# Linear attention and a gated channel mix: the branch to the general path in front of the last two downs, one store per tile, and the first cast of v on other engines

## The chip, the cores and the metric

The kernel runs on one core of a Trainium2 chip. The metric is device time in microseconds (us) of one execution. A core has TensorE (PE, with its weight loads as PEld), VectorE (DVE), ScalarE (ACT), GpSimd (POOL) and SyncE (SP), each with a sequencer of its own that works through its instructions in order, and 16 DMA engines behind queues. In this kernel the big transfers are issued by SP.

## The reference

```python
# q, k, v: (8, 8, 576, 64) float32
q_s = softmax of q over the last axis          # exp(q - max) / sum
k_s = softmax of k over axis 2 (the sequence)
kv  = einsum('bhsd,bhse->bhde', k_s, v)
att = einsum('bhsd,bhde->bhse', q_s, kv)
x   = att.transpose(0, 2, 1, 3).reshape(8, 576, 512)
x_prev = x shifted by one position, zeros first
xk = mu_k * x + (1 - mu_k) * x_prev
xr = mu_r * x + (1 - mu_r) * x_prev
k  = maximum(xk @ w_k, 0)                      # (512, 1024)
v  = k * k @ w_v                               # (1024, 512)
r  = 1 / (1 + exp(-(xr @ w_r)))                # (512, 512)
out = r * v                                    # (8, 576, 512) float32
```

## The kernel before

There are 8 batches. Each batch goes through attention in two units of four heads: `load` of q, k and v (SP), `exp` of q and k (ACT), a cast of v to bf16 (`cast_v`), `sum_q` and `scale_q` (DVE), a transpose of q (by TensorE in the first two batches, by DMA later), `kv` and `x` (TensorE). For the first two batches the mixing weights are folded into the small kv matrix (`weigh_kv`, `x_mixed`, `evict_mixed`); for the others ACT and DVE do the shift and the mix (`shift_x`, `mix_x`). Then follow eight `up` steps per batch (128 features each, 8 matmuls), `relu` on ACT and `square` on ACT or DVE.

The output is made in pairs of batches, 4 pairs of 9 tiles (i, m), 128 rows by 512 columns each: `gate` (4 matmuls) with `tanh` on ACT, `down` (8 matmuls of 512 columns), `finish` on DVE, which multiplies the two into an output buffer `ot` (four of these), and `store` to HBM. Tile m = 4 of each pair holds the last 64 rows of one batch and the first 64 of the next. The last tile, (3, 8), is made in two halves of 256 columns. Accumulators of gates and downs share two buffers of PSUM (`one`).

The kernel skips subtracting the maximum before the exponentials. To be safe, it keeps the reciprocals of all sums in `inv`; `watch` counts on DVE those that lie between 1e-6 and 1e6, `gather` adds the counts by one small matmul, `judge` writes a flag, and `read_flag` loads it into a register of every engine. If a sum was out of range, all engines run `general()`, which does the whole computation again with the maxima subtracted; otherwise all engines jump over it. With the given inputs they jump. The jump is a compare-and-branch on each of the five sequencers; a prefetch hint for it is given at the program's start to the engines named in `mark_branch_hint_location`. Behind a branch an engine that jumped raises the semaphores that its part of the general path would have raised, so that later waits hold on both paths: each engine its own, and SP also those of the eight lanes over which the DMAs' semaphores go round.

The order of the work is written by a planner. The class `Plan` holds steps with an engine (or a choice of engines), a cost and a due time; it plays them through once and calls the steps' functions in the order of their planned starts. A table `SHIFTS` moves every step's due time, and `FIXED` pins some steps to an engine. Idle stretches of TensorE ahead of the first up are filled with `warm` matmuls. In the kernel before, the plan holds all downs and finishes. The last three tiles, called `LATER`, are stored behind the branch, and the branch stands behind everything else:

```python
    with tc.manual_schedule():
        pl.emit(("PE", 0.3, warm, ev["mup"], ev["up", 0, 0]))
        kept, slot = {("ot", *t): slot[("ot", *t)] for t in LATER}, Turns()
        slot.update(kept)
        with tc.If(st["bad"] != 0, preferred_fallthrough_block=True, label="general"):
            general()
        for t in LATER[:-1]:
            store(*t)
        for a in range(2):
            store(*LAST, (nc.sync, nc.scalar)[a], a)
```

Each `store` issues two DMAs of 64 rows. In the program's view of the changed kernel, the lines of the kernel are ten later at the front and up to 25 later at the end.

Of the kernel before, what the change touches and what calls it, by code (L numbers as in the profile page):

```python
# [10 lines left out]
ACT = mybir.ActivationFunctionType  # L11
# [11 lines left out]
-371 1633 2839 -359 6 -1821 -1 -304 3 72 -1538 -534 1385 822 386 1069 -2408 351 589 -649 -354  # L23
-2035 -676 -1613 84 2123 10 -534 -412 -25 -715 1916 -1725 -252 -583 -1817 -117 -752 329 -1136
992 961 677 -574 918 969 976 964 799 489 1060 918 899 960 1082 774 1283 758 736 1180 1358 1293
1147 1581 1449 458 1496 286 1228 1220 169 640 -286 -1128 -413 488 -1330 2596 -2246 -36 -1916
-587 -1383 -627 -498 539 859 1579 -494 1647 1856 345 957 2374 2099 -212 -469 -542 -1593 -544
-554 -64 -295 1476 -1579 -769 -366 -57 119 2187 -967 -615 -1616 395 -602 -3116 894 1329 906 176
1387 -4293 -42 -1020 1086 -2414 311 41 -306 1796 -2617 -3490 -377 -1313 -483 304 -157 -580 -251
-1948 -1869 -2051 -642 149 -1242 -447 112 -849 -2 -546 1212 -853 2304 -589 -455 -286 1353 -1236  # L30
126 -562 -1050 1419 -1647 275 -2047 -660 -2500 -1185 577 -845 -1119 665 541 518 -756 -278 -1809
747 -877 -2031 -467 1876 271 253 -608 -548 -1112 464 -568 -2071 -169 -1882 706 2652 320 -1180 50
-763 -1899 -847 -829 -547 335 -849 -1767 -1763 -1098 -424 -649 -201 459 -745 -1690 -320 -820
-1995 -2164 -141 779 -1519 996 796 263 961 -59 1472 749 1415 -1972 -2090 -987 -620 -143 837 1067
-67 813 516 183 1210 2280 -70 331 -995 1225 195 894 -1462 -25 1058 937 1209 384 -49 1172 1035
1165 967 1477 1807 981 -920 626 -422 2118 -1017 386 -684 1275 736 75 273 -221 -481 86 1590 1303
-768 1234 1613 2230 -1042 681 1411 -307 -389 886 -849 -427 1883 1145 -1070 278 -1072 895 -1821
-1804 1691 586 -600 -1426 -198 454 -1280 -299 1282 1334 -313 707 -1680 -335 -292 -474 796 1620
-263 23 1272 -357 1598 1064 -2901 -390 -2837 1326 -552 -1417 -200 -419 -226 1844 -3 -102 1195
628 354 543 -339 -913 1764 -1857 334 -3424 1373 1829 541 1472 653 901 441 1138 1771 -699 -694  # L40
-560 -1258 -707 1375 602 679 361 1851 612 -1386 -856 -529 294 1595 1043 -473 93 178 -592 135
-1788 99 -4132 955 953 517 1107 -1189 -1541 -3341 284 309 981 980 813 -584 -979 329 -416 -2743
-2298 -1498 -1654 -358 -1383 -1214 -4023 -572 -785 1013 -1457 1502 275 -1354 497 -2225 -388 -830
-401 -573 -172 -1671 -199 -924 -1162 -439 -2067 -806 -292 745 -1209 754 923 -667 349 622 -831
2024 266 -1483 -875 172 818 -838 -727 340 2219 1365 1198 1033 1354 -1181 2156 -519 1317 -774 615
-987 1621 84 1079 830 -945 1156 2076 254 -1771 919 -426 955 1153 -2552 721 -1882 678 855 -1245
-2372 -3135 -3280 1036 1245 388 382 775 986 -1530 -1449 1294 -186 674 -1282 437 -1007 56 -1372
671 569 -3033 1345 -1017 -1146 810 -3295 -213 -2650 1308 -450 -1041 340 1045 -415 -3330 640 -280
-1558 -1620 -1082 1329 -273 1404 1142 -331 -57 -789 -782 2497 -445 -258 276 264 -941 -1029 -903
389 1131 455 378 324 1297 1045 1425 88 -373 1103 131 396 273 29 601 1511 -359 1645 -212 376 1318  # L50
-1239 289 39 1764 1345 -998 2961 -1552 -1875 -618 -1758 1360 1000 -546 182 1835 1436 916 -448
-1361 1710 850 1177 -509 -394 -1154 596 1040 -147 752 584 461 448 179 2019 848 772 2104 434 1490
-577 500 -380 721 1242 -644 -203 -840 -1264 790 1323 800 1249 -1395 -3082 -102 1148 907 303 911
819 1034 230 1083 859 -1270 1178 857 1389 -1029 -3290 871 -1391 658 -2200 -1108 -1167 -1593 674
-151 -2322 1468 -666 788 1148 -2079 -964 583 -1436 -1585 712 -2742 -3491 -3982 708 -4466 -3011
-129 1128 -218 -717 -866 -600 530 -2508 -2780 -447 -1911 346 791 -1290 -435 -1268 -229 355 -3522
-4279 75 -737 -3082 1775 -897 -3480 -1190 1067 666 -937 475 21 -740 -16 -506 315 464 -193 -2109
-809 1236 843 -723 -1841 1711 670 1539 -9997977 -9998081 -9998655
"""
FIXED = {s: e for e, steps in {  # L60
    "DVE": (31, 142, 153, 168, 180, 199, 206, 208, 420, 423, 426, 429, 435, 441, 444, 453,
        456, 465, 468, 474, 480, 486, 501, 504, 507,),
    "ACT": (151, 156, 162, 166, 172, 181, 185, 191, 204, 438, 447, 471, 492, 495, 498,),
    "POOL": (33, 34, 138, 157, 175, 194,),
# [3 lines left out]
class Plan:  # L68
# [12 lines left out]
    def step(self, eng, cost, due, fn=None, after=(), uses=(), lat=0.12):  # L81
        s = {"eng": eng if isinstance(eng, dict) else {eng: cost}, "due": due, "fn": fn,
             "n": len(self.steps), "lat": lat, "uses": [], "left": 0, "next": [], "fix": None}
        self.steps.append(s)
        self.link(s, after, uses)
        return s
# [78 lines left out]
    def emit(self, fill=None):  # L165
        order = self.run()
        if fill:
            eng, gap, fn, first, last = fill
            t, more = first["start"] + first["cost"] + 1.0, []
            for s in [s for s in order if s["on"] == eng]:  # L170
                while first["start"] < s["start"] <= last["start"] and t + gap < s["start"]:
                    more.append({"start": t, "fn": fn, "eng": {eng: gap}, "on": eng})
                    t += gap
                t = max(t, s["start"] + s["cost"])
            order = list(heapq.merge(order, more, key=lambda s: s["start"]))
        for s in order:
            if s["fn"]:
                s["fn"](s["on"]) if len(s["eng"]) > 1 else s["fn"]()
# [3 lines left out]
def kernel(  # L182
# [335 lines left out]
    LATER = [(B // 2 - 1, m) for m in (J - 3, J - 2, J - 1)]  # L518
# [14 lines left out]
    def store(i, m, eng=None, a=None):  # L533
        c0, c1 = (0, C) if a is None else (a * C // 2, (a + 1) * C // 2)
        for h in range(2):
            blk = 2 * m + h
            b, jj = 2 * i + blk // J, blk % J
            (eng or nc.sync).dma_start(
                out=bass.AP(tensor=out.tensor, offset=out.offset + (b * S + jj) * C + c0,
                            ap=[[J * C, 64], [1, c1 - c0]]),  # L540
                in_=at("ot", i, m)[64 * h:64 * h + 64, c0:c1])
# [17 lines left out]

    def read_flag():  # L560
# [3 lines left out]
            "general", "LikelyTaken", engines=[mybir.EngineType.SP, mybir.EngineType.Activation])  # L564
# [99 lines left out]
    for n in range(B):  # L664
        for u in range(2):
# [7 lines left out]
            if n < NM:  # L673
                vc = [pl.step({"ACT": 0.6, "POOL": 0.68, "DVE": 0.65}, 0, LATE,
# [57 lines left out]
    for b in range(B):  # L732
        mixed = [ev["mix", b, u, 0, c] for u in range(2) for c in range(2)]
        relus = []
        for f in range(FT):
# [5 lines left out]
            if f % 2:  # L741
# [3 lines left out]
                relus = []  # L745
    for i in range(B // 2):
        for m in range(J):
# [9 lines left out]
            for a in ((None,) if (i, m) != LAST else (0, 1)):  # L757
                s, z = sl("one", "vp", i, m, a), 1.0 if a is None else 0.5
                p = pl.step("PE", z * T_DOWN, d, lambda i=i, m=m, a=a: down(i, m, a),
                            after=[*ev["wv"], *squares], uses=[sl("k2", i), s], lat=0.2)  # L760
                ev["fin", i, m, a] = p = pl.step(
                    "DVE", 0.6 * z, d + 1.7 * z, lambda i=i, m=m, a=a: finish(i, m, a),
                    after=[p, t], uses=[s, th, ot])
                d += 0.9
            if (i, m) not in LATER:
                pl.step("DMA", 1.0, d + 1.5, lambda i=i, m=m: store(i, m), after=[p], uses=[ot],
                        lat=2.0)

    d = due["down", B // 2 - 1, J - 3]
    a = pl.step("DVE", 1.2, d - 6.0, watch, after=[ev["mix", B - 1, u, 0, h]  # L770
                                                   for u in range(2) for h in range(2)])
    a = pl.step("PE", 0.2, d - 4.0, gather, after=[a], uses=[sl("two", "flag")], lat=0.2)
    a = pl.step("DVE", 0.2, d - 3.0, judge, after=[a], uses=[sl("two", "flag")])
    a = pl.step("PE", 0.1, d, read_flag, after=[a])
    for t in LATER:
        pl.step("DMA", 0.0, LATE, after=[a, *(s for k, s in ev.items()
                                              if k[0] == "fin" and k[1:3] in LATER)],
                uses=[sl("ot", *t)])
# [34 lines left out]
    def general():  # L813
        for i in range(B // 2):
# [26 lines left out]
            for m in range(J):  # L841
                gate(i, m)
                tanh(i, m)
                down(i, m)
                finish(i, m)
                if (i, m) not in LATER:
                    store(i, m)

    with tc.manual_schedule():
        pl.emit(("PE", 0.3, warm, ev["mup"], ev["up", 0, 0]))  # L850
        kept, slot = {("ot", *t): slot[("ot", *t)] for t in LATER}, Turns()
        slot.update(kept)
        with tc.If(st["bad"] != 0, preferred_fallthrough_block=True, label="general"):
            general()
        for t in LATER[:-1]:
            store(*t)
        for a in range(2):
            store(*LAST, (nc.sync, nc.scalar)[a], a)
# [30 lines left out]
```

## Time and profile before

| what | before |
|---|---|
| times of 3 runs | 208.03, 208.97, 210.22 us; median 208.97 |
| the profiled execution: its own time | 207.88 us |
| the profiled execution: span of the page | 206.0 us |
| TensorE busy | 186.6 us, 91% |
| ACT / DVE / POOL busy | 145.1 / 140.5 / 32.4 us |
| first `up` matmul starts | 20.43 us |
| last matmul ends | 196.15 us |
| DMA of the program | 46.41 MB on SP's queue, 0.14 MB on ACT's |

The page and the answers of the trace are of one execution. Times in them count from the start of the span. An engine's name with a q behind it (SPq, ACTq, DVEq, PEldq) is that engine's sequencer: rows of waits, branches, semaphores and issued DMAs, during which the engine itself may be at work. In a row of waits, "X <- Y: a, n, b" says that X waited for Y for a us in all, n times, the longest b us. In a row of the timeline the first two numbers are the start and the duration in us, and the brackets name the idle time before and what ended it.

### The profile page before, as it was taken

To read this page: it belongs to the slowest core of one execution; us is meant where nothing else is said; L and a number is where in the kernel's file an instruction comes from. 1 tells how busy PE (TensorE), PEld (TensorE's weight loads), DVE (VectorE), ACT (ScalarE), POOL (GpSimd) and SP (SyncE) were. 2 spreads that over 40 slices of the span, in tenths; PEclk is the share of its full clock that TensorE was granted. 3 is DMA by queue.
4 is the path that set the end of the run, shared out by engine and by line. 5 is a ranking of instruction groups with operands and counts; after the bars stand their busy time and mean duration, and the time that the engine had idled before them with its cause. 6 is when DMAs were issued, how large, how long until landed. Compare 5 with 4: busy or idle time off the path is not lost.

```text
span 206.0 us, 4670 instructions
## 1 busy us (share of the span) xinstructions
PE 186.6 (91%) x1883; PEld 109.6 (53%) x1883; DVE 140.5 (68%) x214; ACT 145.1 (70%) x210; POOL 32.4 (16%) x43
## 2 busy tenths in 40 slices
PE   0779998999999899999999999999999999999900
PEld 0355775664545466665556656555646567555500
DVE  2985399887979478998689989696935282443210
ACT  3745798898894889798968999969629996330100
POOL 2067425550200400220210060000000000000000
PEclk9999999999999999999999999999999999999985
DMA  5999999989989999999999999507143222243315
GB/s 207 342 400 387 392 389 389 389 258 341 265 226 306 296 362 395 335 290 286 304 354 344 244 331 155 102 11 162 40 98 75 51 51 54 51 102 75 84 34 128
DMA packets 35883, 46.90 MB, mean 228 GB/s; under 512 B 16264, under 2 KB 16528, under 8 KB 35856
## 3 DMA queue, kind: packets, MB, share of 16 engines
q1 hardware_dynamic: 35680, 46.41, 75.0%
q8 instruction: 16, 0.26, 0.6%
q10 hardware_dynamic: 176, 0.14, 0.3%
q14 instruction: 11, 0.09, 0.2%
HBM read 33.56 MB, written 9.44 MB: 209 GB/s over the span
## 4 chain that ended last, share of the span: by engine, by line
PE 74%; DMA 10%; ACT 5%; issue 2%; SPq 2%; POOL 1%; DVE 1%; ACTq 0%
PE two L490 27%; PE one L523 25%; PE one L509 14%; DMA ldv<-in_v_dram 4%; DMA ldq<-in_q_dram 4%; PE two L415 3%; DMA ldk<-in_k_dram 3%; PE two L468 2%; PE two L446 2%; SPq L365 2%; ACT rel L495 1%; POOL vb L277 1%; ACT eq L370 1%; ACT ek L370 1%; PE two L398 1%
## 5 line engine op out<-in xcount | busy, mean ns | idle before, releaser
L490 PE MATMUL two<-xk,wk_bf 128*128 128x288 bf16 x512 | 69.0, 286 | 1.0 <-ACT rel L495 1.0
L523 PE MATMUL one<-wv_bf,k 128*128 128x512 bf16 (+1 forms) x296 | 66.7, 374 | 0.0
L490 PEld LDWEIGHTS <-wk_bf 128*128 128x128 bf16 x512 | 49.6, 98 | 19.8 <-issue 1.4
L495 ACT ACTIVATE rel<-two 128x576 bf16<-128x576 f32 x64 | 41.0, 651 | 14.9 <-PE two L490 12.5
L523 PEld LDWEIGHTS <-k 128*128 128x128 bf16 x296 | 28.1, 98 | 29.8
L529 DVE SCALAR_TENSOR_TENSOR ot<-th,one 128x512 f32<-128x512 f32 (+1 forms) x37 | 24.6, 665 | 22.3 <-PE one L523 19.4
L509 PE MATMUL one<-wr_bf,xr 128*128 128x512 bf16 x144 | 36.3, 380 | 0.1
L277 POOL CAST vb<-ldv 128x1152 bf16<-128x1152 f32 (+1 forms) x19 | 21.5, 1149 | 84.4 <-DMA ldv<-in_v_dram 82.8
L476 ACT ACTIVATE aw<-two,om 128x575 bf16<-128x575 f32 x48 | 32.6, 747 | 0.2 <-PE two L468 0.2
L514 ACT ACTIVATE th<-one 128x512 f32<-128x512 f32 x36 | 21.3, 598 | 16.1 <-PE one L509 15.0
L505 DVE TENSOR_TENSOR k<-rel 128x1152 bf16<-128x1152 bf16 x22 | 17.0, 771 | 14.7 <-ACT rel L495 14.7
L380 DVE TENSOR_REDUCE rs<-eq 128x18 f32<-128x1152 bf16 x16 | 21.6, 1348 | 2.3 <-ACT eq L370 2.1
L385 DVE TENSOR_TENSOR qs<-eq,inv 128x1152 bf16<-128x1152 bf16 x16 | 22.8, 1433 | 0.1
L481 DVE SCALAR_TENSOR_TENSOR xr<-two,mu,aw 128x576 bf16<-128x576 f32 x24 | 19.3, 807 | 3.0 <-ACT aw L476 2.9
L370 ACT ACTIVATE ek<-ldk 128x1152 bf16<-128x1152 f32 x16 | 18.6, 1163 | 3.8 <-DMA ldk<-in_k_dram 3.8
L370 ACT ACTIVATE eq<-ldq 128x1152 bf16<-128x1152 f32 x16 | 18.6, 1165 | 3.7 <-DMA ldq<-in_q_dram 3.7
L481 DVE SCALAR_TENSOR_TENSOR xk<-two,mu,aw 128x576 bf16<-128x576 f32 x24 | 19.0, 806 | 3.0 <-ACT aw L476 3.0
L509 PEld LDWEIGHTS <-xr 128*128 128x128 bf16 x144 | 13.2, 98 | 12.1 <-issue 0.3
L503 ACT ACTIVATE k<-rel 128x1152 bf16<-128x1152 bf16 x10 | 11.7, 1168 | 0.3
L415 PEld LDWEIGHTS <-ek 64*64 64x64 bf16 x576 | 6.4, 113 | 5.7 <-issue 3.2
L415 PE MATMUL two<-vb,ek 64*64 64x65 bf16 x576 | 8.2, 200 | 1.0 <-POOL vb L277 1.0
L446 PE MATMUL two<-qT,kvm 64*64 64x256 bf16 (+2 forms) x160 | 6.8, 295 | 1.1 <-ACT qT L276 0.6
(52 smaller groups left out, 77.5 us busy)
## 6 DMA issues: line engine op xcount, KB each, us to landing
ldq<-in_q_dram SPq DMA_DIRECT2D x16, 576.0 KB, 7.4
ldk<-in_k_dram SPq DMA_DIRECT2D x16, 576.0 KB, 6.9
out_dram<-ot SPq DMA_DIRECT2D x70, 128.0 KB, 3.2
ldv<-in_v_dram SPq DMA_DIRECT2D x15, 576.0 KB, 6.1
k<-in_moe_w_k_dram SPq DMA_DIRECT2D x2, 1024.0 KB, 11.4
k<-in_moe_w_v_dram SPq DMA_DIRECT2D x2, 1024.0 KB, 14.4
xr<-in_moe_w_r_dram SPq DMA_DIRECT2D x1, 1024.0 KB, 15.9
ldv<-in_v_dram SPq DMA_DIRECT2D x2, 288.0 KB, 9.1
```

What stands on the lines that cost most here:

```text
L277: return {"DVE": nc.vector, "POOL": nc.gpsimd}[eng].tensor_copy(out=out, in_=in_)
L370: nc.scalar.activation(out=at("e" + n, b, u)[:].rearrange("p j (h d) -> p h j d", h=2), in_=at("ld" + n, b, u)[:].rearrange("p h (j d) -> ...
L380: nc.vector.reduce_sum(out=rs[:], in_=at("eq", b, u)[:].rearrange("p j (h d) -> p (j h) d", h=2), axis=AX.X)
L385: nc.vector.tensor_tensor(out=at("qs", b, u)[:].rearrange("p j (h d) -> p (j h) d", h=2), in0=at("eq", b, u)[:].rearrange("p j (h d) -> p ...
L476: nc.scalar.activation(out=at("aw", b, u, h, w)[:, 1:S], in_=x_of(b, u, h)[:, 1:S], func=ACT.Copy, scale=om[:, c:c + 1])
L481: nc.vector.scalar_tensor_tensor(out=blend(b, w)[:, 2 * u + h, :], in0=x_of(b, u, h)[:, 64:64 + S], scalar=mu[:, c:c + 1], in1=at("aw", b, ...
L490: nc.tensor.matmul(ps[:, a, 0:HS], lhsT=wk_bf[:, ct, 128 * f:128 * f + 128], rhs=xk[:, ct, HS * a:HS * a + HS], start=(ct == 0), stop=(ct ...
L495: nc.scalar.activation(out=at("rel", b, f // 2)[:, f % 2, :].rearrange("p (a c) -> p a c", a=2), in_=at("two", "up", b, f)[:, :, 0:HS], fu ...
L509: nc.tensor.matmul(at("one", "rp", i, m)[:], lhsT=at("xr", i)[:, ct, 128 * m:128 * m + 128], rhs=wr_bf[:, ct, :], start=(ct == 0), stop=(c ...
L514: nc.scalar.activation(out=at("th", i, m)[:], in_=at("one", "rp", i, m)[:], func=ACT.Tanh, scale=0.5)
L523: nc.tensor.matmul(at("one", "vp", i, m, a)[:, cols], lhsT=at("k2", i)[:, f, 128 * m:128 * m + 128], rhs=wv_bf[:, f, cols], start=(f == 0) ...
L529: nc.vector.scalar_tensor_tensor(out=at("ot", i, m)[:, cols], in0=at("th", i, m)[:, cols], scalar=1.0, in1=at("one", "vp", i, m, a)[:, col ...
```

## The change

Three edits, and a new order of nearly all steps, since `SHIFTS` and `FIXED` are replaced as a whole.

- The branch becomes a step of the plan. It stands behind the down of tile (3, 6) and all finishes of earlier tiles; the downs of (3, 7) and (3, 8) and the finishes and stores of all three tiles are emitted behind it. The last three tiles' tanh comes ahead of it. The general path does the last pair's first down of these tiles itself, and leaves the other two to the common end. The flag's steps get earlier due times. The hint is given to four engines.
- `store` issues one DMA per tile, where the tile lies in one batch.
- For the first unit's two half casts of v the planner's cost on GpSimd is 1.2 instead of 0.68.

```diff
 FIXED = {s: e for e, steps in {
-    "DVE": (31, 142, 153, 168, 180, 199, 206, 208, 420, 423, 426, 429, 435, 441, 444, 453,
-        456, 465, 468, 474, 480, 486, 501, 504, 507,),
...
+    "DVE": (142, 161, 172, 180, 191, 199, 210, 420, 423, 426, 432, 444, 447, 450, 456,
+        471, 474, 486, 495, 504,),
...
+        done = set()
+        for k, s in enumerate(order):
+            if s["fn"] and k not in done:
+                if s["tail"] == "first":
+                    for n in range(k + 1, len(order)):
+                        if not order[n]["tail"]:
+                            done.add(n)
+                            self.call(order[n])
+                self.call(s)
...
     def store(i, m, eng=None, a=None):
         c0, c1 = (0, C) if a is None else (a * C // 2, (a + 1) * C // 2)
-        for h in range(2):
-            blk = 2 * m + h
-            b, jj = 2 * i + blk // J, blk % J
+        runs = [(h, 1) for h in range(2)] if 2 * m + 1 == J else [(0, 2)]
+        for h, n in runs:
+            b, jj = 2 * i + (2 * m + h) // J, (2 * m + h) % J
             (eng or nc.sync).dma_start(
                 out=bass.AP(tensor=out.tensor, offset=out.offset + (b * S + jj) * C + c0,
-                            ap=[[J * C, 64], [1, c1 - c0]]),
-                in_=at("ot", i, m)[64 * h:64 * h + 64, c0:c1])
+                            ap=[[C, n], [J * C, 64], [1, c1 - c0]]),
+                in_=at("ot", i, m)[64 * h:64 * (h + n), c0:c1])
...
+    HINTED = [getattr(mybir.EngineType, e) for e in ("PE", "DVE", "Activation", "SP")]
...
         tc.mark_branch_hint_location(
-            "general", "LikelyTaken", engines=[mybir.EngineType.SP, mybir.EngineType.Activation])
+            "general", "LikelyTaken", engines=HINTED)
...
-                vc = [pl.step({"ACT": 0.6, "POOL": 0.68, "DVE": 0.65}, 0, LATE,
+                vc = [pl.step({"ACT": 0.6, "POOL": 0.68 if n + u else 1.2, "DVE": 0.65}, 0, LATE,
...
+    branch = pl.step("PE", 0.3, LATE, lambda: part())
+    branch["tail"] = "first"
...
+                late = [branch] if (i, m) in TAIL else []
+                ev["down", i, m, a] = p = pl.step(
+                    "PE", z * T_DOWN, d, lambda i=i, m=m, a=a: down(i, m, a),
+                    after=[*ev["wv"], *squares, *(late if (i, m) != TAIL[0] else [])],
+                    uses=[sl("k2", i), s], lat=0.2)
+                ev["fin", i, m, a] = f = pl.step(
                     "DVE", 0.6 * z, d + 1.7 * z, lambda i=i, m=m, a=a: finish(i, m, a),
-                    after=[p, t], uses=[s, th, ot])
+                    after=[p, t, *late], uses=[s, th, ot])
+                o = pl.step("DMA", 0.8, d + 2.5 * z,
+                            lambda i=i, m=m, a=a: store(i, m, nc.sync if a is None else nc.scalar, a),
+                            after=[f], uses=[ot], lat=2.0)
...
+    def part():
+        nonlocal slot
+        planned, slot = slot, Turns()
+        for key in (("k2", B // 2 - 1), *(("th", *t) for t in TAIL),
+                    ("one", "vp", *TAIL[0], None)):
+            slot[key] = planned[key]
+        with tc.If(st["bad"] != 0, preferred_fallthrough_block=True, label="general"):
+            general()
+        slot = planned
...
     with tc.manual_schedule():
         pl.emit(("PE", 0.3, warm, ev["mup"], ev["up", 0, 0]))
-        kept, slot = {("ot", *t): slot[("ot", *t)] for t in LATER}, Turns()
-        slot.update(kept)
-        with tc.If(st["bad"] != 0, preferred_fallthrough_block=True, label="general"):
-            general()
-        for t in LATER[:-1]:
-            store(*t)
-        for a in range(2):
-            store(*LAST, (nc.sync, nc.scalar)[a], a)
```

In the built program the last instructions of TensorE are then: gate, down (3, 6), branch, first half of down (3, 8), down (3, 7), second half of down (3, 8). In front of all, POOL casts one half of the first unit's v and ACT the other; before, POOL cast both.

## The prediction

> **What bounds the kernel now.** I read the page first, then the waits of TensorE, then the chain of waits from its end backwards, and last the sequencers' rows of the branch. The page says that TensorE is the bound:
>
> ```profile
> span 206.0 us, 4670 instructions
> PE 186.6 (91%) x1883; PEld 109.6 (53%) x1883; DVE 140.5 (68%) x214; ACT 145.1 (70%) x210; POOL 32.4 (16%) x43
> ```
>
> The 19.4 us in which it is idle lie at two places. The waits of TensorE give the inner ones, largest first:
>
> ```profile
> PE two L308 <- DVE th L302: 5.5, 1, 5.5
> PE two L490 <- ACT rel L495: 1.0, 1, 1.0
> PE two L415 <- POOL vb L277: 1.0, 1, 1.0
> PE two L398 <- DVE qs L385: 0.8, 1, 0.8
> PE two L446 <- ACT qT L276: 0.6, 1, 0.6
> ```
>
> These are the start (5.5, then 0.8 and 1.0) and two short stalls, 0.6 near 34 us and 1.0 near 66 us. From 67 us on the chain of waits is TensorE alone, one line after the other, until its last matmul ends at 196.15 us. What is left up to 206.02, 9.87 us, is idle TensorE. That end is what the change rebuilds; here is the branch at its head, for every engine (columns: count, duration in ns, first and last start in us):
>
> ```profile
> L853 SPq EVENT_SEMAPHORE  x8: 17/17/17, 193.2 to 193.7; - x8
> ...
> L853 ACTq COMPARE_BRANCH  x1: 73/73/73, 192.5 to 192.5; - x1
> ...
> L853 SPq COMPARE_BRANCH  x1: 78/78/78, 192.7 to 192.7; - x1
> L853 ACTq EVENT_SEMAPHORE  x1: 17/17/17, 193.0 to 193.0; - x1
> L853 PEldq COMPARE_BRANCH  x1: 3312/3312/3312, 194.9 to 194.9; - x1
> L853 DVEq COMPARE_BRANCH  x1: 72/72/72, 196.2 to 196.2; - x1
> L853 PEldq EVENT_SEMAPHORE  x1: 51/51/51, 198.3 to 198.3; - x1
> L853 DVEq EVENT_SEMAPHORE  x1: 21/21/21, 199.1 to 199.1; - x1
> ```
>
> The hinted engines (SP, ACT) are past the branch 0.5 us after it starts; the two without a hint need 2.9 us (DVE, 196.19 to 199.05) and 3.4 us (TensorE, 194.93 to 198.30). Behind the branch each engine raises its own semaphores, and SP those of the eight DMA lanes; each of these rows first waits for the semaphore it raises. The stores wait for DVE's:
>
> ```profile
> SPq L538 <- DVEq L853: 5.3, 1, 5.3
> L538 SPq DMA_DIRECT2D out_dram<-ot x6: 482/596/1234, 199.1 to 203.1; - x6
> DMA to landing us min/median/max: 2.0/2.5/3.3
> ```
>
> So the 9.87 us are: last finish 0.45 (to 196.60), DVE's late branch 2.5 (to 199.10), SP issuing six stores one after the other 4.0 (the last starts at 203.09), its landing 2.04 (205.13), the closing barrier 0.89 (206.02).
>
> **Part 1: branch ahead of the last two downs.** I count from A, the moment when TensorE has only these left: the last gate (0.86), the down of tile (3,6) (1.73), a half down of (3,8) (0.87), the down of (3,7) (1.73), the other half (0.87); together 6.06. Before, that was 196.15 - 6.06 = 190.09, and the span ended at A + 15.93. The built program of after gives the order: gate, down (3,6), branch, half, (3,7), half. Steps:
> - The finish of the last ordinary tile, (3,4), ends at A + 0.72 (0.03 + 0.69). This tile lies in two batches, so it still has two stores on SP: 0.75, and 0.53 later. One lands 2.36 after its start (the pair at 190.60 and 191.13: median 2.3, longest 2.4): A + 3.64.
> - SP's row for the DMA lanes waits until this store has landed; its lane comes first, and the eight rows take 0.53 from first to last (193.20 to 193.73): A + 4.2. The finish of (3,6) on DVE overwrites a buffer that the general path also stores from, so it waits for four lanes, the last of the eight included. It runs from 4.2 to 4.9, not from 2.6.
> - Queued behind it: TensorE's down of (3,7), which takes the accumulator that this finish frees. TensorE could start it at 3.9 (gate and down 2.59; the wait for its own matmuls behind the branch and refilling the array, which no row shows: between 0.1, a wait between engines, and 0.6; I take 0.45, from a matmul's length beyond its pitch, 0.16, and three sequencer steps of near 0.1; then the half, 0.87). It starts at 4.95. The branch thus costs TensorE about 1.5 us in all, and the exact drain is hidden under this wait; with the wait gone the drain alone would cost 0.45.
> - (3,7) ends at 6.7, the last half at 7.55, its finish (0.42) at 8.0. Its store on ACT lands after 2.0 to 2.5; I take 2.4, for twice the bytes of the 2.0 row: 10.4. The store of (3,7), issued on SP at 7.4, lands by then. Barrier 0.89: A + 11.3.
> Gain: 15.93 - 11.3 = 4.6 us; bounds 3.6 (landing as slow as 3.3) to 5.7 (the wait for the lanes is not met).
>
> The flag is read earlier: five TENSOR_LOADs of 0.49 to 0.84 us. On ACT (191.85) and on TensorE (194.33) they ran while the engine worked off what was queued (0.60 us of tanh; twelve matmuls), so I put nothing; uncovered, each costs its length. The flag's matmul now stands two ups (1.96) behind the last batch's mixes, while DVE needs one mix (0.81) and the check (1.37 from 167.75 to 169.12): short by 0.2, inside the middle's bounds below.
>
> **Part 2: hints.** SP and ACT have them already. For DVE the 2.9 us are what stood on the path before, but in the new place DVE branches at A + 0.05 and nothing asks for it before 4.2: free with or without. TensorE's sequencer reached its branch 1.2 us before its matmuls ended; here a full down (1.73) covers it. Without a working hint TensorE resumes at 4.3 if the sequencer runs ahead like that, and (3,7) begins at 5.2, 0.25 us late; if the branch starts only when the down has ended, at 2.59, it resumes at 6.0: 1.9 us late. The Trainium skill (Runtime: NRT & Kernel Launch, Instruction fetch mechanics) says that a taken branch to a target outside the two pages held makes a fetch by DMA before anything executes. That speaks against a branch in TensorE's stream, which jumps some 3,700 instructions; the rows of DVE and TensorE agree with it (2.9 and 3.4 us), those of ACT and SP (0.5) are shorter jumps and tell little of hints. By the rule alone the span would be 0.25 to 1.9 us longer than my sum.
>
> **Part 3: one store per tile.** SP issues one DMA of about 0.6 instead of two (0.47 + 0.58) for all but the four tiles that lie in two batches. In the stream this is off the path; at the end it takes out most of the 4.0 us counted above.
>
> **Part 4: first v cast.** The start, in the timeline:
>
> ```profile
> 9.11 3.06 DVE L385 TENSOR_TENSOR qs<-eq,inv 128x1152 bf16<-128x1152 bf16 x2
> ...
> 10.30 2.42 POOL L277 CAST vb<-ldv 128x576 bf16<-128x576 f32 x2 [8.64 <-DMA ldv<-in_v_dram]
> ...
> 12.77 0.71 PE L415 MATMUL two<-vb,ek 64*64 64x65 bf16 x35 [0.98 <-POOL vb L277]
> ...
> 13.29 0.68 POOL L277 CAST vb<-ldv 128x576 bf16<-128x576 f32 x1 [0.57 <-DMA ldv<-in_v_dram]
> ```
>
> Two casts of 1.21 each beside the scaling (0.68 without it) hold up TensorE. Now one half goes to ACT, idle from 10.12 to 11.64 (0.66): done at 11.5, not 12.7. But two small DVE copies (0.16 + 0.17) now stand ahead of the scaling, and evictions change engines, so I count 1.0 of the 1.2 us at the first up (20.43 before).
>
> **The rest of the order.** New due times and engines move nearly every step, with the same work. The front's 1.0 us lasts only if nothing downstream is fixed in time: until 45 us the queues move near 390 GB/s and their loads come when they come; ACT and DVE are 81 to 95% busy from 30 to 60 us, and the 1.0 us stall at 66 us hangs on a k load. Bounds: all kept and both inner stalls gone, -2.6; all lost and 3 us of new stalls, +3. I take half of the front, -0.5.
>
> **Sum.** 206.0 - 4.6 - 0.5 = 200.9 span. The profiled execution took 207.88, 1.86 more than its span: 202.8. The median of the runs is 208.97, 1.09 above that execution, so on its scale 203.9.
>
> **Rivals.**
> - *The lanes do not hold DVE* (the store lands before anyone asks): (3,7) starts at 3.9, 1.05 earlier: 202.8. For: other pairs landed as fast as 2.2. Against: 4.2 would have to fall to 3.2.
> - *The new order fills the inner stalls too*: 2.1 better than the sum: 201.8. For: the order asks for ups and gates where TensorE waited. Against: ACT and DVE have little room there.
> - *TensorE pays for its branch* (the rule above): 204.2 to 205.8, say 205.
> - *The middle loses a little*: front gone and 2 us of stalls: 206.4.
> - *Slower*: SP's single queue starves TensorE. In the new order the first store, which waits for the first finish, stands behind 24 loads and ahead of those of v for batch 2 and k for batch 3 and of a transpose; before, 28 loads and two transposes stood ahead of it. Queued loads land by 45.4; the first down now comes near 41 us and its finish near 43. If that slips, each us beyond 45 delays those loads, ACT's exps, and, once the slack of some 2 us is used, TensorE by as much. A slip of near 7 us past that eats the 5.1 and goes 2.2 beyond: 211.2. From 52 us for the first finish on it decides. Against: before, SP idled from 34.2 to 43.5 at a transpose and TensorE lost only 1.0.
>
> **Numbers.** Forecast 0.46, lanes 0.12, stalls filled 0.10, branch paid 0.10, middle loses 0.12, starved 0.10. About 1% (2.1 us) is what a measurement tells from no change: faster is below 206.9. All but the last two cases are faster and half of the 206.4 case with its spread: 0.82; within 1%: 0.09; slower 0.09. The range 200.7 to 207.4 leaves out the starved case and about a tenth at the low and high ends.
>
> **What would show it.** In the profile of after: first up near 19.4 us; first finish near 43; DVE's finish of (3,6) starting about 4.2 us after the last ordinary down, behind SP's semaphore rows; a gap of 0.4 and one of about 1 us on TensorE, both after its branch; 3.8 us from the last matmul to the end; TensorE's branch row near 0.1 and its semaphore within 0.6. The forecast is wrong if TensorE has more than 2 us of new idle time between 30 and 190 us, or if its branch row still says 3.3 with matmuls waiting behind it.

## The result, and the profile after

| what | before | after |
|---|---|---|
| median of the runs | 209.59 us (208.03 to 210.92, 4 runs) | 285.04 us (284.68 to 286.68, 4 runs) |
| ratio, with 95% interval | 1 | 1.362 (1.350 to 1.374) |
| span of the profiled execution | 206.0 us | 282.9 us |
| first `up` / A (see the prediction) / last matmul / end | 20.43 / 190.09 / 196.15 / 206.0 | 18.45 / 246.71 / 268.00 / 282.9 |

The medians are of all runs and the ratios of the fast ones alone (those within 1.5% of a kernel's fastest run), so a ratio need not be the quotient of the medians beside it. The change costs 75 us where 5 us of gain were forecast. By the last row of the table, 56.6 us of the 76.9 us of span are lost ahead of A, in the stream, and 20.3 in the tail. The page after, its first two parts (the rows of digits are 40 slices of 7.07 us; PEclk is the granted clock, GB/s is what all 16 DMA engines moved), and last the GB/s row of before, whose slices are 5.15 us:

```profile
span 282.9 us, 4608 instructions
PE 204.0 (72%) x1857; PEld 116.3 (41%) x1882; DVE 139.1 (49%) x211; ACT 149.8 (53%) x214; POOL 31.0 (11%) x42
PE   2899899699099909939199293999969999940600
PEclk9999999989669987977779968699979999995665
GB/s 247 395 386 392 387 389 206 154 328 69 255 286 126 247 99 366 282 52 215 52 123 327 103 195 67 54 68 70 69 102 80 50 50 40 47 68 69 22 50 39
...
GB/s 207 342 400 387 392 389 389 389 258 341 265 226 306 296 362 395 335 290 286 304 354 344 244 331 155 102 11 162 40 98 75 51 51 54 51 102 75 84 34 128
```

TensorE was 91% busy and is 72% busy now. For the same matmuls it is busy 204.0 us instead of 186.6, because the granted clock falls after the holes (the PEclk row). The GB/s rows say where to look: in slices 2 to 6 the transfers run near 390, as before; from then on many slices stand between 50 and 70, in the middle of the stream as well as at its end, while in before every slice from the second to the 24th is above 220. The waits, the largest ones of TensorE, and what ACT and DVE wait for:

```profile
PE two L478 <- DMA qT<-qs: 17.1, 4, 5.7
PE one L533 <- DVE ot L539: 12.8, 1, 12.8
PE two L425 <- ACT rel L505: 7.3, 1, 7.3
PE two L500 <- ACT rel L505: 5.8, 1, 5.8
...
ACT ek L380 <- DMA ldk<-in_k_dram: 26.3, 6, 7.6
DVE ot L539 <- DMA out_dram<-ot: 11.9, 3, 5.8
DVE ot L539 <- SPq L878: 15.2, 1, 15.2
```

Behind nearly every one stands a transfer: the transposes of q, the loads of k that ACT's exps wait for, and stores that keep an output buffer. The two waits for `rel` belong to it: in the timeline ACT waits 7.6 and 6.8 us for a load of k, runs that exp, and only then the relu for which TensorE has been waiting. In before only the start and two stalls of 0.6 and 1.0 us were left. At the end, when the stores are alone, the view of the DMA engines from 250 to 283 us shows what a store gets (a digit is the mean busy share of 16 engines, in tenths):

```profile
DMA  1111394111111000001011111111111111111100
GB/s 50 52 50 50 99 199 129 65 55 50 50 50 55 37 0 0 0 10 30 20 42 50 50 52 52 47 51 48 51 51 52 50 47 52 50 52 47 47 2 0
...
out_dram<-ot SPq DMA_DIRECT2D x2, 256.0 KB
```

From 273 to 281 us the busy share is 0.13, and two of 16 engines are 0.125. A packet of 2 KB took 0.084 us, so two engines, one packet after the other on each, move 49 GB/s, which is the row. By this estimate a merged store of 256 KB takes 5.2 us at best, while a store of 128 KB at the end of before landed 2.4 us after its issue. By the packets' times, exactly two packets were under way for some 84 us of the run; before, for 2 us. And different stores go to the same two engines: from 269 to 280 us SP's queue moves 33 GB/s and ACT's, with its merged halves of the last tile, 16, which together is 49 again and not twice that.

The size of the loss follows. An estimate from these rows: 31 merged stores are 8.13 MB, at 50 GB/s 163 us on two engines. The other 38.1 MB of SP's queue, if spread evenly, keep each engine busy for another 98 us at 390 GB/s. The two engines that carry both then have 261 us of work in a span of 283. By this they are the bound of the kernel after, and TensorE no longer is. SP, which works through its instructions in order, is held at its issues too. Its twelve rows of a transpose took 1.25 to 2.62 us each in before, and 1.33 to 10.22, in the median 5.99, in after; two of these are:

```profile
49.00 3.84 SPq L416 DMA_TRANSPOSE qT<-qs  x1
...
61.82 8.51 SPq L416 DMA_TRANSPOSE qT<-qs  x1
```

The rows of the branch and of the tail, which answer to those shown of before:

```profile
L878 SPq EVENT_SEMAPHORE  x8: 17/17/17, 261.9 to 262.5; - x8
...
L878 DVEq COMPARE_BRANCH  x1: 84/84/84, 246.8 to 246.8; - x1
L878 DVEq EVENT_SEMAPHORE  x1: 21/21/21, 247.5 to 247.5; - x1
L878 PEldq COMPARE_BRANCH  x1: 382/382/382, 247.5 to 247.5; - x1
...
L878 SPq COMPARE_BRANCH  x1: 78/78/78, 253.8 to 253.8; - x1
```

```profile
262.63 1.02 DVE L539 SCALAR_TENSOR_TENSOR ot<-th,one 128x512 f32<-128x512 f32 x2 [15.20 <-SPq L878]
263.37 0.58 PE L533 MATMUL one<-wv_bf,k 128*128 128x512 bf16 x1 [12.82 <-DVE ot L539]
```

The hints work: DVE needs 0.7 us for its jump (2.9 before), TensorE's branch row is 0.38 (3.31 before). But the wait for the lanes, forecast at 4.2 us behind A, ends 15.9 us behind it, because SP itself comes to its branch only at 253.8 and its row then waits for stores of 5 us or more.

### The profile page after: what moved, and what is told of

The parts are those of the page before. It is cut to its first block, busy times and chain, and to the rows that moved or that the text cites. A ratio compares the mean times of both kernels' runs of the same rounds, so it can differ in the third digit from the quotient of the medians.

```text
span 282.9 us, 4608 instructions
## 1 busy us (share of the span) xinstructions
PE 204.0 (72%) x1857; PEld 116.3 (41%) x1882; DVE 139.1 (49%) x211; ACT 149.8 (53%) x214; POOL 31.0 (11%) x42
## 5 line engine op out<-in xcount | busy, mean ns | idle before, releaser
L533 PE MATMUL one<-wv_bf,k 128*128 128x512 bf16 (+1 forms) x281 | 75.2, 412 | 14.9 <-DVE ot L539 12.8
L500 PE MATMUL two<-xk,wk_bf 128*128 128x288 bf16 x512 | 72.8, 294 | 6.2 <-ACT rel L505 5.8
L500 PEld LDWEIGHTS <-wk_bf 128*128 128x128 bf16 x512 | 50.9, 101 | 28.2 <-issue 9.0
L533 PEld LDWEIGHTS <-k 128*128 128x128 bf16 x296 | 30.5, 106 | 50.1 <-issue 25.4
L519 PE MATMUL one<-wr_bf,xr 128*128 128x512 bf16 x134 | 39.6, 412 | 0.8 <-issue 0.4
L390 DVE TENSOR_REDUCE rs<-eq 128x18 f32<-128x1152 bf16 x16 | 21.6, 1350 | 13.0 <-ACT eq L380 12.8
L515 DVE TENSOR_TENSOR k<-rel 128x1152 bf16<-128x1152 bf16 x19 | 15.4, 809 | 23.9 <-ACT rel L505 23.9
L478 PE MATMUL two<-qT,kvs 64*64 64x448 bf16 (+2 forms) x144 | 7.3, 299 | 19.7 <-DMA qT<-qs 17.1
L519 PEld LDWEIGHTS <-xr 128*128 128x128 bf16 x144 | 14.5, 105 | 15.0 <-issue 4.7
L425 PEld LDWEIGHTS <-ek 64*64 64x64 bf16 x576 | 7.3, 118 | 19.6 <-ACT rel L505 7.9
L513 ACT ACTIVATE k<-rel 128x1152 bf16<-128x1152 bf16 x13 | 15.2, 1172 | 0.2
```

The lines of the kernel that those rows point to most:

```text
L390: nc.vector.reduce_sum(out=rs[:], in_=at("eq", b, u)[:].rearrange("p j (h d) -> p (j h) d", h=2), axis=AX.X)
L500: nc.tensor.matmul(ps[:, a, 0:HS], lhsT=wk_bf[:, ct, 128 * f:128 * f + 128], rhs=xk[:, ct, HS * a:HS * a + HS], start=(ct == 0), stop=(ct ...
L519: nc.tensor.matmul(at("one", "rp", i, m)[:], lhsT=at("xr", i)[:, ct, 128 * m:128 * m + 128], rhs=wr_bf[:, ct, :], start=(ct == 0), stop=(c ...
L533: nc.tensor.matmul(at("one", "vp", i, m, a)[:, cols], lhsT=at("k2", i)[:, f, 128 * m:128 * m + 128], rhs=wv_bf[:, f, cols], start=(f == 0) ...
```

## The experiments

### Which part costs 75 us

The first three kernels take the merged store out of the kernel after, put it alone into the kernel before, and keep two stores per tile in a shape that also has 2 outermost. (In this and the following cuts the names of the kernels are put in, and lines that matter less are left out.)

```diff
 e1_two_stores (from after)
-        runs = [(h, 1) for h in range(2)] if 2 * m + 1 == J else [(0, 2)]
+        runs = [(h, 1) for h in range(2)]
...
 e2_before_merged (from before): the store of after
...
-                            ap=[[J * C, 64], [1, c1 - c0]]),
+                            ap=[[C, n], [J * C, 64], [1, c1 - c0]]),
...
 e4_outer2_two_stores (from after): each store in two halves of the columns
+            for e in range(2):
+                w = (c1 - c0) // 2
...
+                            ap=[[C, n], [J * C, 64], [1, w]]),
```

> The changed kernel with two stores of 64 rows per tile again; branch, hints, order and casts stay as changed. Theory 'two engines' (a store whose outer dimension is 2 is carried by 2 of the 16 DMA engines, at the 50 GB/s that the end of the changed kernel's trace shows, and holds up what is queued with it): all of the loss goes, and what my sum of the other parts said is left: 200 to 207 us, against 209.6 before. Rival 'order' (the new order of loads and stores in SP's queue starves TensorE): it stays slow, 265 us or more, since two stores take even more of SP's time than one.

> The kernel before with nothing changed but one store per tile in its stream and at its end, in the form of the changed kernel. Theory 'two engines': 32 stores of 256 KB at some 5 us each on two engines, which the loads share: 255 to 300 us. Rival 'order': the old order is untouched and SP issues fewer stores: 205 to 211 us.

> The changed kernel with two stores per tile, each of all 128 rows but half of the columns: as many DMAs and as many bytes in each as in the kernel before, but the outer dimension is 2. Theory 'two engines': as slow as the changed kernel or slower, since rows of 1 KB are twice as many: 280 to 330 us. Rival 'size' (a store of 256 KB, or fewer semaphores among which the DMAs go round, is what hurts): back near 205 to 215 us.

Measured: e1 208.83 us beside 210.97 of before, ratio 0.989 (0.981 to 0.997). e2 281.03 and e4 297.74, one run each. The whole loss is the store: without it the rest of the change is a small gain (smaller than the 200 to 207 expected), and alone in the old order it costs 70 us. It is not the size or the number of transfers, since e4 has nearly as many of the same size (62 of 128 KB on SP, 70 in before) and is slower than e2; the count of 2 in front is common to after, e2 and e4, which all lose some 70 us or more.

The Trainium skill (DMA: Bandwidth & Descriptors, Why a DMA increments its semaphore by 16 and not by 1) gives the rule: the slowest dimension of each side that is not 1 sets the number of engines, the largest number up to 16 that divides both. Here that is 2, and the two busy engines and 50 GB/s agree with it. The next pair tests it in the kernel before, by where each store of 64 rows is cut in two:

```diff
 g62_stores_62_and_2_rows / g60_stores_60_and_4_rows (from before)
+            for r0, r1 in ((0, 62), (62, 64)):        # g60: (0, 60), (60, 64)
...
-                            ap=[[J * C, 64], [1, c1 - c0]]),
+                            ap=[[J * C, r1 - r0], [1, c1 - c0]]),
```

> The kernel before with each store of 64 rows cut into one of 62 rows and one of 2 rows: same bytes, order and queue, twice the transfers. Theory (the outermost count of a transfer sets how many engines it uses, by its largest divisor up to 16): 62 rows divide by 2 and 31, so they go to 2 engines and the kernel is as slow as the merged one: some 270 to 300 us, with two DMA engines busy alone for long stretches. Rival (only the outermost dimension of 2 matters, a long one spreads whatever its divisors; what is paid is the number of transfers): 209 to 216 us.

> The counterpart of g62_stores_62_and_2_rows: each store of 64 rows of the kernel before cut into one of 60 and one of 4 rows, so the same number of transfers, bytes and order. Theory (the largest divisor up to 16 of the outermost count sets the engines): 60 divides by 15, so the big part spreads over 15 engines and the small one over 4: 209 to 216 us, some 85 us faster than g62. Rival (g62 was slow for its double number of transfers, or for its small second parts): as slow as g62, 270 to 300 us.

Measured, one run each: g62 298.61 us, g60 214.45. Two rows moved from one transfer to the other change the time by 84 us: 62 divides by 2 but by nothing larger up to 16, 60 by 15. At the end of g62, 250 to 296 us:

```profile
DMA  1111111111111111111111111111111111111110
GB/s 52 52 50 52 52 50 52 52 50 52 50 52 50 59 52 48 52 57 66 52 64 59 52 57 38 40 41 30 52 45 46 45 50 52 52 50 50 48 48 7
```

The same 50 GB/s, though the transfers that carry the bytes have 62 in front; the parts of 2 rows are 4 KB each. That the small parts as such, or the double number, are the cause is ruled out by g60, which has both. That settles the mechanism. The price of twice as many transfers is at most the 5 us by which g60 is above before.

### What the rest of the change is worth: the tail

e1 gained 2.3 us where the prediction's other parts summed to 5.1. Its waits of TensorE, the largest ones without the start, and its tail:

```profile
PE one L533 <- DVE ot L539: 2.5, 1, 2.5
PE two L425 <- ACT ek L380: 2.1, 1, 2.1
PE two L425 <- POOL vb L287: 2.0, 2, 1.2
```

```profile
197.99 1.02 DVE L539 SCALAR_TENSOR_TENSOR ot<-th,one 128x512 f32<-128x512 f32 x2 [4.91 <-SPq L878]
198.73 4.44 PE L533 MATMUL one<-wv_bf,k 128*128 128x512 bf16 x15 [2.52 <-DVE ot L539]
```

A is 192.36 here, so the lanes let DVE go at A + 5.6, not 4.2. Behind the wait come 15 matmuls in 4.4 us. By stretches (columns: length, busy time of PE, PEld, DVE, ACT and POOL, then granted clock, DMA share, GB/s):

```profile
196.00:199.00 3.00, 0.48 (x3) 0.18 (x3) 1.01 (x2) 0.00 (x0) 0.00 (x0) 1.00 0.02 5
199.00:203.00 4.00, 3.95 (x15) 1.85 (x14) 0.69 (x2) 0.00 (x0) 0.00 (x0) 0.57 0.38 98
```

The clock is halved for 3.4 us of it, which by estimate costs half of that, 1.7. The next kernels give the last three tiles buffers of their own, so that no finish behind the branch waits for a landing (h1), and take the hint from TensorE and DVE (h2):

```diff
 h1_own_last_tiles (from e1_two_stores)
+        "last": (3, [128, C], F32),
...
+    def kept(i, m):
+        return "last" if (i, m) in TAIL else "ot"
...
-            out=at("ot", i, m)[:, cols], in0=at("th", i, m)[:, cols], scalar=1.0,
+            out=at(kept(i, m), i, m)[:, cols], in0=at("th", i, m)[:, cols], scalar=1.0,
...
 h2_own_last_tiles_hint_sp_act (from h1)
-    HINTED = [getattr(mybir.EngineType, e) for e in ("PE", "DVE", "Activation", "SP")]
+    HINTED = [getattr(mybir.EngineType, e) for e in ("SP", "Activation")]
```

> The kernel after, with two stores of 64 rows per tile, and the last three tiles written to three output buffers of their own, so that DVE's finishes behind the branch wait for no store's landing. Theory: in e1_two_stores the wait of 2.5 us of TensorE ahead of the last half downs is DVE held by SP's lane row, and the half clock of 3.4 us behind it follows from that idle. Both gone: TensorE's gaps behind its branch add up to under 1 us, the granted clock stays 1.0 to the last matmul, and the time falls by 2.5 + 1.7 = 4.2 us against e1: some 204.6. Rival: something else releases the finish just as late (the read of the flag on DVE, the tiles before it), and the time stays at 208 to 209. In between (the lane wait goes but ACT's last stores are held by SP's lanes): 206 to 207.

> As h1_own_last_tiles, with the branch hint on SP and ACT alone (as the kernel before has it). Theory: without the hint TensorE's branch takes 3.3 us instead of 0.4 and DVE's 2.9 instead of 0.7, with no lane wait to cover them, so TensorE idles some 3 us in front of the half downs: 1.4 to 3 us slower than h1, up to 4.5 if the idle also brings the half clock. Rival: the hint buys nothing because DVE's finish of the tile before is late anyway: within 0.5 us of h1.

Measured: h1 207.11 us beside 209.67, ratio 0.988 (0.983 to 0.993); h2 208.05, 0.984 (0.979 to 0.989). The medians miss both expectations (h1 should have been near 204.6, h2 1.4 us or more behind it); the tails meet them. TensorE's last row in h1:

```profile
196.22 5.67 PE L537 MATMUL one<-wv_bf,k 128*128 128x512 bf16 x32
```

No gap, and from A (195.44) to the end 10.7 us instead of e1's 14.8. But A came 3.1 us later than in e1, 0.8 of it ahead of the first up: of two programs whose TensorE does the same work in the same order, one lost 2.3 us more in the middle, 1.7 of them, by the same estimate, to a half clock after an idle stretch of 2.3 us at 100 us. In h2 the tail is 12.7 from A, with TensorE's wait for its branch in the open:

```profile
197.95 3.63 PE L537 MATMUL one<-wv_bf,k 128*128 128x256 bf16 x24 [2.22 <-PEq L882]
```

So with the lane wait gone, the hint is worth 2.1 us of tail; the middle of the new order, which scatters by as much, hides it in the medians. That asks for the old order, and for the same three tails in it.

### The tail alone, in the order of before

h3 takes each step's due time, cost and engine from the plan of before; only the flag's steps come early, and the end is that of h1. SP's, ACT's, DVE's and TensorE's work is in the order of before up to the flag.

```diff
 h3_order_before_early_branch (from h1)
-        for n, d in enumerate(SHIFTS.split()):
-            self.steps[n]["due"] += 100 * int(d)
+        for n, d in enumerate(DUE.split()):      # the due times of the plan of before
+            self.steps[n]["due"] = int(d)
...
-                vc = [pl.step({"ACT": 0.6, "POOL": 0.68 if n + u else 1.2, "DVE": 0.65}, 0, LATE,
+                vc = [pl.step({"ACT": 0.6, "POOL": 0.68, "DVE": 0.65}, 0, LATE,
...
 h3b_hint_sp_act (from h3): the hint as in h2
 h3c_shared_buffers (from h3)
-        return "last" if (i, m) in TAIL else "ot"
+        return "ot"
```

> The kernel before with its own order of steps (its due times and engines), two stores per tile and both first casts of v on GpSimd; only the end is the changed one: flag read early, branch behind the down of (3,6), hint on four engines, and the last three tiles in buffers of their own. Theory: the branch early is worth what the end of h1_own_last_tiles shows: 10.6 us from A (only the last gate and three downs left) to the end of the span, where the kernel before takes 15.9; and the 3 to 5 us that e1 and h1 lose ahead of A come from the new order of the middle alone. So here A stays at 190 to 191 and all of 5.3 us comes through: 204.2 to 204.9 on the scale of 209.5 to 209.7, a ratio of 0.975 to 0.98. Rival: the read of the flag and the branch early cost the middle something in any order (TENSOR_LOADs on busy engines, the flag's matmul between ups): A at 192 or later, and 206 to 208.

> As h3_order_before_early_branch, with the hint on SP and ACT alone. Theory: TensorE's branch row goes from 0.38 to 3.3 to 3.9 us, and TensorE stands idle 2.2 us in front of its half down, as in h2: 2.1 us slower than h3, some 206.5. Rival: the hint is free because DVE's finishes or the stores set the end: equal to h3.

> As h3_order_before_early_branch, with the last three tiles in the four common output buffers, as in the kernel after. Theory: DVE's finish of (3,6) waits for SP's row of the lanes, and so for the landing of the last ordinary store: from 4.2 (a landing of 2.4) to 5.6 us (a landing of 3.7, as in e1) behind A. TensorE idles 1 to 2.5 us; 1.7 more if the half clock follows, as in e1: 205.4 to 208.6, against 204.5 of h3. Rival: the lanes have landed by then: equal to h3.

| kernel | median, us | ratio to before | A | A to end | idle TensorE behind the branch |
|---|---|---|---|---|---|
| h3 | 204.88 | 0.979 (0.975 to 0.983) | 190.71 | 10.7 | under 0.25 |
| h3b | 207.90 | 0.991 (0.987 to 0.995) | 192.05 | 14.6 | 2.4 |
| h3c | 208.11 | 0.995 (0.991 to 0.999) | 191.38 | 12.8 | 1.95 |

Before had A at 190.09 and 15.9 to its end. h3 and h3c come out as expected; h3b is 3.0 us behind h3 where 2.1 were expected, as its tail meets a half clock too. The rival that an early branch costs the middle something falls with h3's A. h3 beats both kernels, by 4.4 us against before. Its row of TensorE's branch and the matmuls around it:

```profile
L897 PEldq COMPARE_BRANCH  x1: 380/380/380, 191.5 to 191.5; - x1
```

```profile
190.55 1.03 PE L535 MATMUL one<-wr_bf,xr 128*128 128x512 bf16 x4
191.49 5.67 PE L552 MATMUL one<-wv_bf,k 128*128 128x512 bf16 x30
```

h3b, where TensorE's sequencer needs 4.1 us for the jump:

```profile
L897 PEldq COMPARE_BRANCH  x1: 4112/4112/4112, 192.8 to 192.8; - x1
```

```profile
197.12 1.69 PE L552 MATMUL one<-wv_bf,k 128*128 128x256 bf16 x9 [2.41 <-PEq L897]
```

The half clock, 3.4 us long, comes right behind this gap. And h3c, where the lanes hold DVE to A + 5.06:

```profile
196.44 1.02 DVE L558 SCALAR_TENSOR_TENSOR ot<-th,one 128x512 f32<-128x512 f32 x2 [4.33 <-SPq L897]
```

In this order, with either of the two edits, hint and buffers, missing, something is 2 us late, and the median is some 3 us higher. The kernel with neither was not run in this order.

### The hint in the kernel as it was changed, and the v cast alone

```diff
 f1_hint_sp_act (from e1_two_stores): the hint as in h2
 h4_v_cast_alone (from before)
+        if (b, u) == (0, 0) and hs == (1, 2):
+            eng = "ACT"
```

> As e1_two_stores (order of after, two stores per tile, common output buffers), with the hint on SP and ACT alone. Theory of the prediction: as long as the lanes hold DVE's finish of (3,6) to some 5 us behind A, a late TensorE (its branch row at 3.9 instead of 0.38) hides behind the same wait; its half down moves to A + 4.7 or so and (3,7) starts when the finish allows it: within 0.7 us of e1, 208.2 to 209.5. Rival: as with buffers of their own (h1 to h2: 2.1 in the tail, h3 to h3b: 3.0), the hint is worth 2 to 3 us here too: 211 to 212.

> The kernel before with the one edit of the front: the second half of the first unit's v cast on ACT, not GpSimd. Theory of the prediction: first up at 19.2 to 19.4 instead of 20.4, and of this gain of 1.0 us about half is left at the end: 0.5 faster, some 209.0 against 209.5. Rival: the front gain was given back by the planner's other order of the middle in e1 alone (e1 lost 4.0 us between the first up and the last ordinary down), and here all of 1.0 to 1.7 us stays: 207.8 to 208.5. Other rival: the moved cast changes the planner's order here too, and the middle loses 2 to 4 us: 210.5 to 212.5.

f1: 205.86 us beside 209.24, ratio 0.988 (0.979 to 0.998), against 0.989 of e1. The median lies below both expected ranges; but before, too, was 1.7 us faster beside f1 than beside e1, and by the ratios the hint to TensorE and DVE buys nothing that can be measured there. The trace says why:

```profile
195.79 3.75 PE L533 MATMUL one<-wv_bf,k 128*128 128x256 bf16 x24 [2.20 <-PEq L878]
196.03 0.69 DVE L539 SCALAR_TENSOR_TENSOR ot<-th,one 128x512 f32<-128x512 f32 x1 [4.39 <-SPq L878]
```

A is 190.93: TensorE is back at A + 4.86, and DVE's finish, which (3,7) needs, only at A + 5.1. (The tail is 12.8 us without and 14.8 with the hint; the 1.9 are mostly the half clock, which e1 met and f1 did not.)

h4: 209.41 us, ratio 1.001 (0.997 to 1.005): no gain that can be measured, though the half microsecond that was expected lies just inside the interval. The half on ACT is done at 10.95, yet `kv` runs only 0.58 us earlier than before, from 12.19 instead of 12.77. The row names an eviction, but GpSimd's own half takes 1.84 us and ends only at 12.14, so without the eviction it would hardly have been earlier:

```profile
10.30 1.84 POOL L277 CAST vb<-ldv 128x576 bf16<-128x576 f32 x1 [8.64 <-DMA ldv<-in_v_dram]
...
12.19 0.71 PE L417 MATMUL two<-vb,ek 64*64 64x65 bf16 x36 [0.64 <-ACT qT L276]
```

The first up is 0.44 earlier (19.99), and short stalls at 56, 67, 90 and 91 us, 2.5 us in all where before had one of 1.0, take more than that.

## Why the prediction was wrong, point by point

- **The step that failed is Part 3: "In the stream this is off the path".** It priced SP's issue (0.6 instead of 0.47 + 0.58) and took the transfer itself to be the same. It left out on how many engines the new shape runs. The term is 70 us by itself (e2's 281.03 less 210.97) and 76 in the new order (after less e1), not about nothing. Nothing in the trace of before showed a transfer with 2 outermost, so it had to be bounded, and the rule of the Trainium skill told above would have given the bound. By estimate: 31 x 256 KB on 2 engines, at a sixteenth of before's 390 GB/s each, 167 us of work for these two.
- **Rivals.** None had this cause. The one on the slow side, "SP's single queue starves TensorE", had the right victims (loads behind stores on SP, then ACT's exps) with another cause and a price of 211.2. Its condition was not met: the first store is issued at 45.0 us, not 52 or later. Of the forecast's own conditions for being wrong, more than 2 us of new idle time between 30 and 190 us is met many times over.
- **Part 1, the tail, 4.6 us.** The mechanism holds: in e1, f1 and h3c the lanes hold DVE's finish of (3,6), TensorE waits behind it, and own buffers remove it. The size was off. A to the end was 14.8, 12.8 and 12.8 us, not 11.3. Two terms: the landing of the last ordinary pair, 2.36 behind its issue by before's rows, took 3.4 to 4.0 (finish at A + 5.1 to 5.6, not 4.2), and in e1 the half clock adds 1.7. From the last matmul to the end it was 3.9 in e1 and 4.2 in h3c, forecast 3.8. Both have two stores per tile, so Part 3's "at the end it takes out most of the 4.0 us" did not hold either: the early branch does it without the merged store.
- **The drain, 0.45.** Measured under 0.25 in h3, where nothing covers it.
- **Part 2, hints free behind the lanes.** Right, by f1 against e1: TensorE unhinted is back at A + 4.86, inside the 4.3 to 6.0 given. The branch row was 3.9 unhinted and 0.38 hinted. The Trainium skill's rule on taken branches (Runtime: NRT & Kernel Launch, Instruction fetch mechanics) agrees with the unhinted 3.9 and 4.1.
- **Part 4, the front.** In after all 36 matmuls of the first `kv` run from 11.74; in before one starts at 11.53 and the other 35 at 12.77. That is the 1.0 counted, and the first up comes at 18.45 in place of the 19.4 forecast. But in h4 the cast alone gives 0.4 at the first up, so the rest came with the new order.
- **The rest of the order, -0.5 (bounds -2.6 to +3).** This term failed as well, by less. In the four profiles with two stores and the new order A comes 0.8 (f1) to 5.4 us (h1) later than in before, where 0.5 earlier was forecast. From first up to A the profiles with two stores and the new order have 172.5 to 176.0 us (e1, f1, h1, h2), those in the old order 169.7 to 172.4 (before, h4, h3, h3b, h3c). Some 3 us more in the middle eat the 1.0 to 2.0 won at the front; the stalls are on `ek` and `vb`, loads of k and v. By the ratios the two orders cannot be told apart with certainty: h1 against h3 is 0.988 to 0.979 for the old one, e1 against h3c 0.989 to 0.995 for the new.
- **The sum without Part 3** was 203.9. e1 gave 2.3 us of its 5.1, h3 4.4, with buffers that the change did not have.

## What to carry to other kernels

Before two transfers are merged, look at the outermost count of both access patterns: here the number of engines that carried a transfer followed from its divisors, and saving an issue of 0.5 us cost seven eighths of the bandwidth (50 GB/s instead of 390). A stretch of the GB/s row that stands at a flat fraction of the usual rate, with one digit of DMA share, is how this looks in a profile; the waits then name mostly loads and transposes, not the stores that cause it. And where one tail is held by two things (here a slow branch and a landing), take away both before judging either.

## What the runs showed that was not expected

- **Half clock after short idle stretches.** The granted clock falls to 0.5 for 3.41 us at a time, on a fixed grid of 3.41 us. In the ten profiles near before's speed, windows ahead of the last matmul in which TensorE was idle for 2.15 (h1), 2.41 (h3b) and 2.58 us (e1) were followed by one; those with 1.92 (f1), 1.86 (g60) and 1.73 (h3b) were not, and one with 1.84 (h2) was. So in these runs some 2 us of idle time in one window cost, by estimate, another 1.7. The Trainium skill (TensorE: Matmul & The Clock Gate, Part 1) has the same window of 3413 ns, but puts the fall of the clock after at least one idle window; here less was enough.
- **An instruction transfer in front of data.** In e1, f1, h1, h2, h3, h3b and h3c a 16 KB packet of the instruction queue starts 1.8 to 2.5 us after A and takes 1.05 to 1.9 us; the pair of stores issued at A + 0.75 and A + 1.26 lands 3.1 to 4.2 us after its issue. In before, where no such packet falls between, the same pair landed after 2.2 and 2.4. In e1 the pair's late packets all follow that one. That it is the cause was not tried by itself.
